# Sliding-window attention and a gated FFN on one core: VectorE's pieces given out behind the gate-value products, and the first batch's attention split between the head and the FFN

## The chip, the core and the metric

The kernel runs on one core of one Trainium2 chip. The metric is the device time of one execution in microseconds. A core has a matrix engine (TensorE, PE in the profile), VectorE (DVE), ScalarE (ACT), GpSimd (POOL) and SyncE (SP, which here only issues DMAs). Each engine runs its own instructions strictly in the order in which they were emitted, and semaphores order them across engines. Matmuls write to PSUM, which has eight banks, and VectorE and ScalarE read the results there.

## The reference

```python
# attention: batch 4, heads 8, sequence 768, head size 64; n_sink 4, window 128
scores = scale * np.matmul(q, k.transpose(0, 1, 3, 2))
keep = is_sink | ((rel >= 0) & (rel < window))      # rel = query position - key position
scores = np.where(keep, scores, -1e9)
a = softmax(scores)
attn_out = np.matmul(a, v)
# FFN: 3072 tokens, d_model 512, d_ff 1536
x = attn_out.transpose(0, 2, 1, 3).reshape(B * S, H * D)
out = (np.maximum(x @ w_gate, 0) * (x @ w_val)) @ w_out
```

A query sees at most 128 keys behind it and the first four keys. The inputs and the output are float32; the kernel multiplies in bf16.

## The kernel before

**Attention.** Two heads form a unit U[i]; a batch has four units, so there are sixteen. Four kinds of step do a unit's attention:

- `T(u)` turns the unit's keys and queries with TensorE (L228), twelve 128x128 transposes. ScalarE copies the keys to `kE` in four pieces and adds the sink keys in a fifth small copy (L233 to L238); VectorE copies the queries to `qT` (L235).
- `Sg(u, g)` computes the scores of key group g (0, 1 or 2) into a two-bank PSUM tile `PP` (L258), and ScalarE takes the exponential into `ee` (L262). The mask is either added beforehand by TensorE (L247, `bias=True`, batch 0) or multiplied in afterwards by VectorE (L264).
- `V(u, part)` multiplies the weights with the values and with ones (L276), for one half of the queries (part 0 or 1). Groups 0 and 1 serve part 0; groups 1 and 2 serve part 1.
- After V, VectorE divides: it transposes the sums (L282), takes the reciprocal (L283), transposes back (L284) and multiplies into `xT` (L286). The multiply is the last reader of V's PSUM tile.

In batches 2 and 3, DMAs turn keys and queries, so `T` is used only for batches 0 and 1.

**FFN.** `F1(b, g, m)` multiplies half g (384 tokens) of a batch with column block m of the gate weights (L302), ScalarE applies the ReLU (L305), then come the value weights (L307) and VectorE's product of gate and value into `hT` (L309). `F2(b, t)` multiplies `hT` with `wo` for 128 tokens (L318), ScalarE copies the result (L320) and a DMA stores it (L321).

**PSUM.** There are two `PP` tiles of two banks, taken in turn by `pair()`, and four single banks `G`, taken in turn by `bank()` for the FFN. In the head (`head[0]`), `two()` gives `T` and `V` two banks of `G`; afterwards it gives them a `PP` tile.

**The order of the work** is written out by hand. The head does all of batch 0's attention. Then come slots: 18 for a batch, twelve with a pair of F1 (both halves of one m; the first four slots of batch 0 pair differently) and six with an F2. The attention of batch b + 1 is put after the slots of batch b's FFN: `events(i)` makes seven steps for a pair of units, and `places` says after which slots they come. `before` holds what is emitted ahead of a slot: loads on SP, casts to bf16 on POOL (`cast_kq`, `cast_v`, `cast_w`, `cast_wo`), and for batches 2 and 3 the DMA transposes. Weights come through three staging tiles `ws`.

VectorE's masks and divisions are emitted at once, in `Sg` and in `V`:

```python
if not bias:
    nc.vector.tensor_tensor(x, x, msk..., op=Alu.mult)
```

Of the kernel before, what the change touches and what calls it, by code (L numbers as in the profile page):

```python
# [11 lines left out]
Alu = mybir.AluOpType  # L12
# [9 lines left out]
def kernel(  # L22
# [123 lines left out]
    def load_w(m0, m1):  # L146
        for w, dst in ((moe_w_gate, wg), (moe_w_val, wv)):
            st = ws[wsn[0] % NW]
            wsn[0] += 1
            n = (m1 - m0) * 128  # L150
            nc.sync.dma_start(out=st[:, 0:KO * n].rearrange("p (k n) -> p k n", n=n),
                              in_=w.rearrange("(ko ki) n -> ki ko n", ki=128)[:, :, m0 * 128:m1 * 128])
            staged[m0, dst is wv] = st

    def cast_w(m0, m1):
        n = (m1 - m0) * 128
        for m in range(m0, m1):
            for x, dst in enumerate((wg, wv)):
                st = staged[m0, x == 1]
                o = (m - m0) * 128  # L160
                nc.gpsimd.tensor_copy(dst[:, :, m * 128:(m + 1) * 128],
                                      st[:, 0:KO * n].rearrange("p (k n) -> p k n", n=n)[:, :, o:o + 128])
# [47 lines left out]
    head = [True]  # L210

    def pair():
        rot[0] += 1
        return PP[rot[0] % 2]

    def two():
        if head[0]:
            srot[0] += 2
            return G[srot[0] % 4][:], G[(srot[0] + 1) % 4][:]
        x = pair()  # L220
        return x[:, 0, :], x[:, 1, :]

    def T(u):
        t = u.i % NT
        tk, tq = two()
        for x, ps in ((kn[u.i % NC], tk), (qn[u.i % NC], tq)):
            for n in range(NR):
                nc.tensor.transpose(ps.bitcast(BF16)[:, 128 * n:128 * n + 128],  # L228
                                    x[:, n, :, :].rearrange("p h d -> p (h d)"), ident[:])
        vk, vq = (ps.bitcast(BF16)[:, 0:768].rearrange("d (n p) -> d p n", p=128) for ps in (tk, tq))  # L230
        e = kE[t]
        to = lambda ap: ap.rearrange("d (p n) -> d p n", n=NR)
        nc.scalar.copy(to(e[:, 0:126]), vk[:, 0:21])  # L233
        nc.scalar.copy(to(e[:, 130:382]), vk[:, 21:63])
        nc.vector.tensor_copy(to(qT[t][:]), vq)  # L235
        nc.scalar.copy(to(e[:, 386:638]), vk[:, 63:105])
        nc.scalar.copy(to(e[:, 642:780]), vk[:, 105:128])
        nc.scalar.copy(e[:, 126:894].rearrange("d (i c) -> d i c", c=256)[:, :, 0:4],  # L238
                       e[:, 0:4].unsqueeze(1).to_broadcast([128, 3, 4]))

    def Sg(u, g, bias=False):
        t = u.i % NT
        n, segs = SEG[g]
        ps = pair()
# [4 lines left out]
        for x0, q0, c0, c1 in segs:  # L249
            for h in range(2):  # L250
                j = X0.index(x0)
# [11 lines left out]
        if not bias:  # L263
            nc.vector.tensor_tensor(x, x, msk[:, g, 0:n].unsqueeze(1).to_broadcast([128, 2, n]), op=Alu.mult)  # L264
# [3 lines left out]
    def V(u, part):  # L268
        pv, pd = two()
        w, h0 = u.i // 2, 2 * (u.i % 2)  # L270
        segs = VSEG[part]
        for which in range(2):
            for i, (j, g, c0, c1, o0) in enumerate(segs):
                for h in range(2):
# [7 lines left out]
        nc.vector.transpose(out=t1[:], in_=pd[:, 0:CUT])  # L282
        nc.vector.reciprocal(r[:], t1[:].rearrange("p (c e) -> p c e", e=32)[:, :, 0])  # L283
        nc.vector.transpose(out=R[:].rearrange("p (c e) -> p c e", e=32),  # L284
                            in_=r[:].unsqueeze(2).to_broadcast([128, CUT // 32, 32]))
        nc.vector.tensor_tensor(xT[u.b % 2][:, u.p, CUT * part:CUT * part + CUT], pv[:, 0:CUT], R[:], op=Alu.mult)  # L286
        ready[u.b, u.p, part] = True

# [6 lines left out]
    def F1(b, g, m):  # L295
        assert all((b, p, g) in ready for p in range(NP)), (b, g)
        x = xT[b % 2]
        c = slice(CUT * g, CUT * g + CUT)
        n = CUT
        gp, vp = bank(), bank()  # L300
        for ko in range(KO):
            nc.tensor.matmul(out=gp[:, 0:n], lhsT=wg[:, ko, m * 128:(m + 1) * 128], rhs=x[:, ko, c],  # L302
                             start=ko == 0, stop=ko == KO - 1)
        gs = gspool.tile([128, S - CUT], F32, name="gs")
        nc.scalar.activation(gs[:, 0:n], gp[:, 0:n], Act.Relu, bias=0.0, scale=1.0)  # L305
        for ko in range(KO):
            nc.tensor.matmul(out=vp[:, 0:n], lhsT=wv[:, ko, m * 128:(m + 1) * 128], rhs=x[:, ko, c],  # L307
                             start=ko == 0, stop=ko == KO - 1)
        nc.vector.tensor_tensor(hT[:, m, c], gs[:, 0:n], vp[:, 0:n], op=Alu.mult)  # L309
# [13 lines left out]
    with tc.manual_schedule():  # L323
# [3 lines left out]
        for u in (1, 2):  # L327
            load_k(U[u])
            load_q(U[u])
            if u == 1:  # L330
                load_v(0, (0, 1, 2, 3))
        load_v(0, (4, 5, 6))
        cast_kq(U[0])
        T(U[0])
        Sg(U[0], 0, bias=True)
        Sg(U[0], 1, bias=True)
# [3 lines left out]
        load_v(1, range(7))  # L340
        load_w(0, 2)
        T(U[1])
        Sg(U[0], 2, bias=True)
        cast_v(0, 0, 4)
        V(U[0], 0)
        Sg(U[1], 0, bias=True)
        cast_kq(U[2])
        cast_v(0, 4, 7)
        V(U[0], 1)
        Sg(U[1], 1, bias=True)  # L350
        T(U[2])
        Sg(U[1], 2, bias=True)
        V(U[1], 0)
        Sg(U[2], 0, bias=True)
        cast_kq(U[3])
        V(U[1], 1)
        Sg(U[2], 1, bias=True)
        T(U[3])
        Sg(U[2], 2, bias=True)
        cast_v(1, 0, 4)  # L360
        V(U[2], 0)
        Sg(U[3], 0, bias=True)
        cast_v(1, 4, 7)
        cast_w(0, 2)
        load_w(2, 4)
        V(U[2], 1)
        Sg(U[3], 1, bias=True)
        V(U[3], 0)
        Sg(U[3], 2, bias=True)
        V(U[3], 1)  # L370
# [6 lines left out]
        def events(i):  # L377
# [7 lines left out]
        ffn[0][0:4] = [lambda: (F1(0, 0, 0), F1(0, 0, 1)), lambda: (F1(0, 0, 2), F1(0, 0, 3)),  # L385
                       lambda: (F1(0, 1, 0), F1(0, 1, 1)), lambda: (F1(0, 1, 2), F1(0, 1, 3))]
# [5 lines left out]
        at(0, lambda: (cast_w(2, 4), kq_in(4), load_w(4, 8)))  # L392
        at(1, lambda: (cast_kq(U[4]), kq_in(5), load_v(2, range(7))))
        at(2, lambda: cast_w(4, 8))
        at(3, lambda: load_w(8, 12))
        at(5, lambda: (cast_kq(U[5]), cast_v(2, 0, 7), kq_in(6), kq_in(7), load_v(3, range(7))))
        at(6, lambda: (cast_w(8, 12), load_wo(0), load_wo(1), load_wo(2)))
        at(9, lambda: (cast_kq(U[6])))
        at(10, lambda: (cast_v(3, 0, 7), [cast_wo(c) for c in range(3)]))
        at(12, lambda: (cast_kq(U[7]),))  # L400
# [17 lines left out]
        for b in range(1, B):  # L418
            ev = events(NP * b) + events(NP * b + 2)
            if b == 1:  # L420
                places = [3, 4, 5, 6, 7, 8, 10, 11, 12, 13, 14, 15, 16, 17]
            else:
                ev = [f for n, f in enumerate(ev) if n % 7 not in (0, 2)]
                places = [2, 3, 4, 6, 7, 9, 10, 11, 13, 14]
# [3 lines left out]
        for b in range(B):  # L428
            for f in ffn[b]:
# [3 lines left out]
                for x in after.get(s, []):  # L433
                    x()
                s += 1
# [35 lines left out]
```

## Time and profile before

| what | value |
|---|---|
| median of 3 runs | 263.98 us (263.98 to 264.33) |
| the profiled execution | 263.85 us |
| its span, first to last instruction | 261.5 us |
| mean granted TensorE clock | 0.998 |
| PE busy | 243.5 us (93%) |
| DVE busy | 149.5 us (57%) |
| ACT busy | 112.4 us (43%) |
| POOL busy | 78.3 us (30%) |
| first matmul; first F1 matmul | 6.00 us; 30.83 us |
| DMA traffic | 38.18 MB, mean 146 GB/s |

The profile is one execution; its span leaves out 2.35 us around the instructions. A row of a group names the line, the engine, the operation and its tiles, then busy time, the mean of one instruction in nanoseconds, and the idle time of the engine ahead of them with what ended most of it. In a row of waits stand the waiting line, what released it, the total in us, the number of times and the longest. In a timeline stand start, duration and instruction. Buffer numbers are left out, so both `PP` tiles are "pp" and all four banks "g".

### The profile page before, as it was taken

The page shows a single profiled execution, that of the slowest core. Times are in us where ns is not written, and L with a number is a line of the kernel's source. Part 1 is how long each engine was busy: PE and PEld are TensorE (multiplying, and loading weights), DVE is VectorE, ACT ScalarE, POOL GpSimd, SP SyncE. Part 2 cuts the span into 40 slices and gives each one's busy share as a digit, 9 for nine tenths or more (in the row PEclk, how much of TensorE's full clock was granted, in tenths as well). Part 3 has the DMA queues.
Part 4 walks back from the last instruction along what each step waited for, and adds up shares of the span by engine and source line. Part 5 has one row for each costly group of instructions (what it writes and reads, how often), then busy time and mean ns, then how long its engine had stood idle before and what let it go on. Part 6 is the DMA issues. An engine that isn't in the chain of part 4 may idle for free.

```text
span 261.5 us, 5120 instructions
## 1 busy us (share of the span) xinstructions
PE 243.5 (93%) x1988; PEld 140.2 (54%) x1988; DVE 149.5 (57%) x289; ACT 112.4 (43%) x210; POOL 78.3 (30%) x127
## 2 busy tenths in 40 slices
PE   0999699999999979998999999999999999999994
PEld 0455466665645545655554555655564556556443
DVE  4289845697835575869683525869683524444100
ACT  2667335745264426452535136453535133333211
POOL 6776558776711262135001135233000000000000
PEclk9999999999999999999999999999999999999999
DMA  6995999999289799920008989930002220000122
GB/s 231 286 285 204 363 335 309 353 292 335 39 180 243 148 231 212 165 37 3 0 3 195 224 189 231 185 70 3 1 0 83 80 80 3 0 0 3 40 107 95
DMA packets 77319, 38.18 MB, mean 146 GB/s; under 512 B 64368, under 2 KB 70768, under 8 KB 77296
## 3 DMA queue, kind: packets, MB, share of 16 engines
q1 hardware_dynamic: 76880, 37.35, 58.0%
q10 hardware_dynamic: 416, 0.52, 0.6%
q8 instruction: 15, 0.25, 0.4%
q14 instruction: 8, 0.07, 0.1%
HBM read 28.43 MB, written 6.29 MB: 133 GB/s over the span
## 4 chain that ended last, share of the span: by engine, by line
PE 74%; DVE 15%; SPq 3%; issue 2%; DMA 2%; ACT 2%; POOL 0%; DVEq 0%; ACTq 0%; POOLq 0%
PE g L318 23%; PE g L307 21%; PE g L302 20%; DVE R L284 4%; PE pp L258 4%; DVE t L282 4%; PE pp L276 4%; DVE xT L286 3%; DVE hT L309 2%; SPq L105 2%; DMA kf<-in_k_dram 2%; DVE r L283 2%; PE g L276 1%; ACT ee L262 1%; SPq L94 1%
## 5 line engine op out<-in xcount | busy, mean ns | idle before, releaser
L307 PE MATMUL g<-xT,wv 128*128 128x384 bf16 x384 | 78.1, 326 | 3.4 <-DVE hT L309 3.4
L309 DVE TENSOR_TENSOR hT<-gs,g 128x384 bf16<-128x384 f32 x96 | 51.5, 551 | 51.1 <-PE g L307 48.8
L302 PE MATMUL g<-xT,wg 128*128 128x384 bf16 x384 | 78.7, 327 | 2.0 <-DVE xT L286 1.3
L305 ACT ACTIVATE gs<-g 128x384 f32<-128x384 f32 x96 | 46.9, 493 | 71.4 <-DVE hT L309 31.5
L318 PE MATMUL g<-wo,hT 128*128 128x512 bf16 (+1 forms) x300 | 64.4, 371 | 0.0
L307 PEld LDWEIGHTS <-wv 128*128 128x128 bf16 x384 | 37.5, 98 | 30.6 <-issue 6.1
L262 ACT ACTIVATE ee<-pp 128x1010 bf16<-128x1010 f32 (+2 forms) x48 | 44.3, 964 | 12.6 <-PE pp L258 12.6
L302 PEld LDWEIGHTS <-wg 128*128 128x128 bf16 x384 | 35.8, 98 | 25.4 <-issue 2.7
L318 PEld LDWEIGHTS <-hT 128*128 128x128 bf16 x300 | 28.4, 98 | 31.0 <-issue 0.4
L264 DVE TENSOR_TENSOR ee<-ee,msk 128x1010 bf16<-128x1010 bf16 (+2 forms) x36 | 28.1, 789 | 23.0 <-ACT ee L262 22.5
L320 ACT COPY ot<-g 128x512 f32<-128x512 f32 (+1 forms) x24 | 13.8, 576 | 50.1 <-PE g L318 44.6
L117 POOL CAST kn<-kf 128x768 bf16<-128x768 f32 x16 | 13.5, 845 | 34.9 <-DMA kf<-in_k_dram 33.8
L284 DVE STREAM_TRANSPOSE R<-r 128x384 f32<-128x384 f32 x32 | 18.5, 578 | 1.1
L276 PEld LDWEIGHTS <-vn 128*64 128x64 bf16 x288 | 12.6, 110 | 8.9 <-issue 7.6
L282 DVE STREAM_TRANSPOSE t<-pp 128x384 f32<-128x384 f32 x24 | 13.8, 576 | 5.1 <-PE pp L276 4.7
L140 POOL COPY kO<-kE 128x372 bf16<-128x372 bf16 x8 | 4.4, 551 | 40.3 <-DMA kE<-kn 20.4
L258 PE MATMUL pp<-qT,kE 64*128 64x255 bf16 (+4 forms) x176 | 15.1, 255 | 1.0 <-DVE xT L286 0.8
L110 POOL CAST vn<-vf 128x1792 bf16<-128x1792 f32 (+2 forms) x10 | 13.8, 1381 | 5.6 <-DMA vf<-in_v_dram 5.6
L117 POOL CAST qn<-qf 128x768 bf16<-128x768 f32 x16 | 13.8, 862 | 5.5 <-DMA qf<-in_q_dram 4.8
L258 PEld LDWEIGHTS <-kE 64*128 64x128 bf16 x176 | 6.9, 94 | 13.4 <-issue 10.6
L286 DVE TENSOR_TENSOR xT<-pp,R 128x384 bf16<-128x384 f32 x24 | 13.4, 558 | 0.8
L276 PE MATMUL pp<-ee,vn 128*64 128x253 bf16 (+8 forms) x216 | 12.4, 236 | 0.4 <-DVE ee L264 0.4
(60 smaller groups left out, 143.8 us busy)
## 6 DMA issues: line engine op xcount, KB each, us to landing
kf<-in_k_dram SPq DMA_DIRECT2D x16, 384.0 KB, 4.8
vf<-in_v_dram SPq DMA_DIRECT2D x48, 128.0 KB, 4.3
out_dram<-ot SPq DMA_DIRECT2D x23, 256.0 KB, 2.2
qf<-in_q_dram SPq DMA_DIRECT2D x15, 384.0 KB, 5.5
ws<-in_moe_w_out_dram SPq DMA_DIRECT2D x3, 1024.0 KB
ws<-in_moe_w_gate_dram SPq DMA_DIRECT2D x2, 1024.0 KB
ws<-in_moe_w_val_dram SPq DMA_DIRECT2D x2, 1024.0 KB, 8.2
ws<-in_moe_w_gate_dram SPq DMA_DIRECT2D x2, 512.0 KB, 6.7
```

What stands on the lines that cost most here:

```text
L117: copy(dst[:], src[:].rearrange("p h (n d) -> p n h d", d=64))
L258: nc.tensor.matmul(out=ps[:, h, c0:c1], lhsT=lhs, rhs=qT[t][64 * h:64 * h + 64, q0:q0 + c1 - c0], start=not bias, stop=True, skip_group_ch ...
L262: nc.scalar.activation(x, ps[:, :, 0:n], Act.Exp, bias=0.0, scale=scale)
L264: nc.vector.tensor_tensor(x, x, msk[:, g, 0:n].unsqueeze(1).to_broadcast([128, 2, n]), op=Alu.mult)
L276: nc.tensor.matmul(out=(pv, pd)[which][64 * h:64 * h + 64, o0:o0 + c1 - c0], lhsT=lhs, rhs=ee[u.i % NE][:, g, h, c0:c1], start=i == 0, sto ...
L282: nc.vector.transpose(out=t1[:], in_=pd[:, 0:CUT])
L284: nc.vector.transpose(out=R[:].rearrange("p (c e) -> p c e", e=32), in_=r[:].unsqueeze(2).to_broadcast([128, CUT // 32, 32]))
L302: nc.tensor.matmul(out=gp[:, 0:n], lhsT=wg[:, ko, m * 128:(m + 1) * 128], rhs=x[:, ko, c], start=ko == 0, stop=ko == KO - 1)
L305: nc.scalar.activation(gs[:, 0:n], gp[:, 0:n], Act.Relu, bias=0.0, scale=1.0)
L307: nc.tensor.matmul(out=vp[:, 0:n], lhsT=wv[:, ko, m * 128:(m + 1) * 128], rhs=x[:, ko, c], start=ko == 0, stop=ko == KO - 1)
L309: nc.vector.tensor_tensor(hT[:, m, c], gs[:, 0:n], vp[:, 0:n], op=Alu.mult)
L318: nc.tensor.matmul(out=op[:, 0:c1 - c0], lhsT=hT[:, m, t * 128:(t + 1) * 128], rhs=wo[:, m, c0:c1], start=m == 0, stop=m == FM - 1)
```

## The change

- **Pieces.** VectorE's masks, the query copies of `T` and the divisions are no longer emitted at once. They go into a queue `later`; a division is two pieces, `inv` (transpose, reciprocal) and `mul` (transpose back, multiply). `some(1)` emits one piece behind every gate-value product, and `some(2)` emits two behind every slot from 12 to 17 of a batch (the F2 slots). `need(key)` emits pieces up to the one that a later step depends on: before a `PP` tile is taken again, before scores read `qT`, before V reads `ee`, before F1 reads `xT`. In the head everything is emitted at once, as before.
- **Head.** The head does `T` for all four units, one unit ahead, and only groups 0 and 1 and the first query half of each. Group 2 and the second query halves come between the F1's of the first four slots; those slots do the first half's F1 for m = 0 to 7, and the next four slots the second half's. The very first F1 works on m = 0 and 1 together, with the last of the four input blocks at the end.
- **PSUM.** `V` after the head and V(U[3], 0) use a `PP` tile; `T` after the head uses one half of each of two `PP` tiles.
- **Places.** Batch 1's fourteen steps come after slots 3 to 16 instead of 3 to 8 and 10 to 17.
- **Loads and casts.** Weights come in six pieces of 256 columns, gate and value in one staging tile, instead of pieces of 256 and 512 columns with a tile each. Several loads and casts are emitted at other slots, and the head loads U[2]'s keys and queries ahead of the first V tiles.
- **Sink keys.** The small copy within `kE` goes from ScalarE to POOL.

The diff, cut to its core:

```diff
     rot, srot = [0], [0]
     head = [True]
+    later, count, due = deque(), [0, 0], {}
+
+    def put(key, *fns):
+        for f in fns:
+            later.append(f)
+            count[0] += 1
+        for x in key:
+            due[x] = count[0]
+        if head[0]:
+            need(key)
+
+    def need(key):
+        n = max([due.get(x, 0) for x in key])
+        while count[1] < n:
+            some(1)
+
+    def some(n):
+        for _ in range(min(n, len(later))):
+            count[1] += 1
+            later.popleft()()
 
     def pair():
         rot[0] += 1
-        return PP[rot[0] % 2]
+        i = rot[0] % 2
+        need([("pp", i)])
+        return PP[i], ("pp", i)
...
     def T(u):
...
-        tk, tq = two()
+        kk = kq = None
+        if head[0]:
+            tk, tq = two()
+        else:
+            (x, kk), (y, kq) = pair(), pair()
+            tk, tq = x[:, 0, :], y[:, 0, :]
...
-        nc.vector.tensor_copy(to(qT[t][:]), vq)
+        put([("q", u.i), kq], lambda: nc.vector.tensor_copy(to(qT[t][:]), vq))
...
-        nc.scalar.copy(e[:, 126:894].rearrange("d (i c) -> d i c", c=256)[:, :, 0:4],
-                       e[:, 0:4].unsqueeze(1).to_broadcast([128, 3, 4]))
+        nc.gpsimd.tensor_copy(e[:, 126:894].rearrange("d (i c) -> d i c", c=256)[:, :, 0:4],
+                              e[:, 0:4].unsqueeze(1).to_broadcast([128, 3, 4]))
...
         if not bias:
-            nc.vector.tensor_tensor(x, x, msk[:, g, 0:n].unsqueeze(1).to_broadcast([128, 2, n]), op=Alu.mult)
+            put([("e", u.i)], lambda: nc.vector.tensor_tensor(
+                x, x, msk[:, g, 0:n].unsqueeze(1).to_broadcast([128, 2, n]), op=Alu.mult))
...
-    def V(u, part):
-        pv, pd = two()
+    def V(u, part, own=True):
+        need([("e", u.i)])
+        if own:
+            x, key = pair()
+            pv, pd = x[:, 0, :], x[:, 1, :]
+        else:
+            key = None
+            pv, pd = two()
...
+        def inv():
+            nc.vector.transpose(out=t1[:], in_=pd[:, 0:CUT])
+            nc.vector.reciprocal(r[:], t1[:].rearrange("p (c e) -> p c e", e=32)[:, :, 0])
+
+        def mul():
+            nc.vector.transpose(out=R[:].rearrange("p (c e) -> p c e", e=32),
+                                in_=r[:].unsqueeze(2).to_broadcast([128, CUT // 32, 32]))
+            nc.vector.tensor_tensor(xT[u.b % 2][:, u.p, CUT * part:CUT * part + CUT], pv[:, 0:CUT], R[:], op=Alu.mult)
+
         ready[u.b, u.p, part] = True
+        put([key, ("x", u.b, part)], inv, mul)
...
+    def F1(b, g, m, ahead=()):
...
+        need([("x", b, g)])
+        work = [(i, bank(), w) for i in (m, *ahead) for w in (wg, wv)]
...
+                    nc.vector.tensor_tensor(hT[:, i, c], gs[i][:], ps[:, 0:CUT], op=Alu.mult)
+                    some(1)
...
+        T(U[0])
+        T(U[1])
+        Sg(U[0], 0)
+        Sg(U[0], 1)
+        T(U[2])
+        Sg(U[1], 0)
+        Sg(U[1], 1)
+        V(U[0], 0, False)
+        T(U[3])
+        Sg(U[2], 0)
+        Sg(U[2], 1)
+        V(U[1], 0, False)
+        Sg(U[3], 0)
+        Sg(U[3], 1)
+        V(U[2], 0, False)
+        V(U[3], 0)
...
+        first = [lambda: (F1(0, 0, 0, (1,)), Sg(U[0], 2), Sg(U[1], 2), F1(0, 0, 2), V(U[0], 1)),
+                 lambda: (F1(0, 0, 3), Sg(U[2], 2), F1(0, 0, 4), V(U[1], 1), Sg(U[3], 2)),
+                 lambda: (F1(0, 0, 5), V(U[2], 1), F1(0, 0, 6)),
+                 lambda: (V(U[3], 1), F1(0, 0, 7))]
+        ffn[0][0:8] = first + [lambda m=m: (F1(0, 1, m), F1(0, 1, m + 1)) for m in (0, 2, 4, 6)]
...
-                places = [3, 4, 5, 6, 7, 8, 10, 11, 12, 13, 14, 15, 16, 17]
+                places = [3, 4, 5, 6, 7, 8, 9, 10, 11, 12, 13, 14, 15, 16]
...
                 for x in after.get(s, []):
                     x()
+                if s % 18 > 11:
+                    some(2)
                 s += 1
```

## The prediction

> **What bounds the kernel now.** I read the page first: engine shares, the chain that ended last, the groups.
>
> ```profile
> PE 243.5 (93%) x1988; PEld 140.2 (54%) x1988; DVE 149.5 (57%) x289; ACT 112.4 (43%) x210; POOL 78.3 (30%) x127
> PE 74%; DVE 15%; SPq 3%; issue 2%; DMA 2%; ACT 2%; POOL 0%; DVEq 0%; ACTq 0%; POOLq 0%
> L309 DVE TENSOR_TENSOR hT<-gs,g 128x384 bf16<-128x384 f32 x96 | 51.5, 551 | 51.1 <-PE g L307 48.8
> L286 DVE TENSOR_TENSOR xT<-pp,R 128x384 bf16<-128x384 f32 x24 | 13.4, 558 | 0.8
> ```
>
> TensorE carries the span; VectorE is on the chain only where TensorE waits for it. So I need TensorE's idle time and, from its timeline, where each wait falls.
>
> ```profile
> PE g L228 <- POOL kn L117: 6.0, 1, 6.0
> PE g L307 <- DVE hT L309: 3.4, 4, 1.2
> PE g L276 <- ACT ee L262: 1.4, 2, 0.8
> PE g L302 <- DVE xT L286: 1.3, 2, 0.8
> PE pp L258 <- DVE xT L286: 0.8, 2, 0.4
> ```
>
> "Idle" starts after the modelled end of a matmul, so I take lost time from starts. Four gate or value matmuls take 0.65 us from start to start; what exceeds that is lost. After 31 us: 0.46 at 59.27 (second scores wait for a division); 1.66 between 91.32 and 94.93 (batch 1's first gates wait for the last divisions); in batch 1 0.65 at 112.71 and 1.38 at 124.72 (a bank waits for a late gate-value product) and 0.43 at 119.41 (a mask); in batch 2 0.66, 0.18 and 1.37 at the same places; 0.4 at 86.89. So 7.2 us in all is what better placing of VectorE's pieces can win there. The change must keep the waits for a `PP` tile covered, and the timeline around 59 us shows how these go:
>
> ```profile
> 57.18 0.57 DVE L282 STREAM_TRANSPOSE t<-pp 128x384 f32<-128x384 f32 x1
> 57.78 0.23 DVE L283 RECIPROCAL r<-t 128x12 f32<-128x12 f32 x1
> 58.05 0.58 DVE L284 STREAM_TRANSPOSE R<-r 128x384 f32<-128x384 f32 x1
> 58.49 0.39 PE L258 MATMUL pp<-qT,kE 64*128 64x255 bf16 x4
> 58.66 0.56 DVE L286 TENSOR_TENSOR xT<-pp,R 128x384 bf16<-128x384 f32 x1
> 59.27 0.36 PE L258 MATMUL pp<-qT,kE 64*128 64x255 bf16 x6 [0.39 <-DVE xT L286]
> ```
>
> The scores at 59.27 start 0.05 after the division that read their `PP` tile ended (58.66 + 0.56). VectorE had started the two divisions as soon as V's matmuls ended, ahead of both later products.
>
> **The stall the change makes.** In the changed program's instruction order, pieces stand behind the gate-value products, and those still pending for a `PP` tile are forced out when that tile is taken again: behind the product just emitted, whose matmuls are the last on TensorE before the taker. TensorE and VectorE each run in order, so this part is serial. Steps from rows of before: the product starts 0.27 after TensorE has issued its last value matmul (40.58 + 0.65 = 41.23, product at 41.50); 0.47 until the next piece starts (the pair at 44.73 takes 1.02); `inv` (transpose, reciprocal) 0.88 (57.18 to 58.05, rounded); `mul` 0.61 until its multiply starts, which takes 0.56 and frees the tile, 0.47 until the next piece; 0.05 back to TensorE. With E the end of the value matmuls, one forced `mul` frees its tile at E + 0.27 + 0.47 + 0.61 + 0.56 = 1.91, TensorE at 1.96.
>
> - First phase (slots 0 to 3). V(U1,1) after F1(0,0,4) waits for the `mul` of V(U0,1) in the same tile: 1.96 instead of 0.08, so 1.9 lost. V(U2,1) after F1(0,0,5) waits for product, `inv`, `mul`: 2.84, so 2.75 lost. T(U4) takes both tiles after F1(0,0,7): product, `mul`, `inv`, `mul`, that is 0.27 + 0.47 + 1.08 + 0.88 + 0.61 + 0.56 + 0.05 = 3.92, where its second half would start at about 0.41: 3.5 lost. Sum 8.1.
> - Batch 0, rest. Slot 8's second scores and slot 10's T(U6) come one slot after two V's, and have the same four steps: 3.5 each. (The first product's wait is 1.3 earlier, its `inv` ends before the second product, which adds 0.05 that I leave out.) The query copies (L235, 0.96) now stand behind a slot's first product: Sg(U4,0) and Sg(U6,0) may start at (E - 1.3) + 0.27 + 0.47 + 0.96 + 0.05 = E + 0.45 instead of 0.08: 0.35 each. V(U5,1) waits for its last mask, given behind the second product (0.27 + 0.47 + 0.69 = 1.43, asked for at about 0.95): 0.45. Sum 8.2.
> - Batches 1 and 2. V to the next scores is two slots, so four products give one piece each; the last `mul` stands behind the fourth product. With F1's at 1.3: first product E - 3.63, `inv` to E - 2.28, product, `mul` to E - 0.73, product, `inv` to E + 0.62, and only then the fourth product (ready at E + 0.27), so `mul` frees the tile at E + 0.62 + 0.47 + 0.61 + 0.56 = E + 2.26. Scores there would start at E + 0.36: 1.95 lost, twice a batch. With one mask wait of 0.45: 4.35 a batch, 8.7 in both.
>
> Behind each waiting matmul stands the whole rest of TensorE's queue; exponentials and products wait with it. In the second half of batches (slots 12 to 17) no product stands between, and pieces run as now.
>
> **What it removes.** Of the 7.2 us, all but the 0.4 at 86.89 have their cause removed: products come before divisions in batches 1 and 2, V(U7) is one slot earlier so F2 covers its divisions, and 59.27's wait is the one costed anew. That is 6.8 us.
>
> **The head.** Half the scores and half the V's move behind the first products; no matmul is added or dropped. Now F1 starts at 30.83, so with its first two products TensorE would be free at 33.43. In the changed order T(U1) stands before Sg(U0,0), and POOL's small kE copy (was ACT's L238; nearest POOL row L141, 0.19) stands between the casts of two units and waits for ACT:
>
> ```profile
> 6.66 0.83 POOL L117 CAST kn<-kf 128x768 bf16<-128x768 f32 x1
> 7.54 0.31 ACT L237 COPY kE<-g 128x138 bf16<-128x138 bf16 x1
> 8.64 0.61 PE L258 MATMUL pp<-qT,kE 64*128 64x253 bf16 x4 [0.20 <-DVE qT L235]
> ```
>
> The cast at 6.66 moves to about 8.1, its partner ends at 9.7, and scores begin at about 10.4 instead of 7.39. Then ACT (exponential pair 1.84, four copies 0.85) and POOL (copy 0.2, two casts 1.6) alternate: T(U3) at about 17.4, scores of U2 and U3 to 21.6, V(U2,0) to 22.4, V(U3,0) to 23.4; divisions of U2 and U3 at 1.96 each end at 26.35, and the last input rows' matmuls of the first two products (0.65) at 27.0. The rest that stood before: four third scores at 0.73, four V's at 0.75, eight changes at 0.06: 6.4. So 33.4 against 33.43: 0. Bounds: -2.5 if POOL and ACT run tighter and TensorE's early slow time is shorter (transposes take 0.77 for six at 6.0, 0.34 from 11.28), +2.5 if the slow time lasts over the idle gap at 7.4 to 9.0, or a V tile's cast is late.
>
> **DMAs.** SP's order changes (U2's keys before V's tiles; weights as twelve 512 KB loads, gate and value of one piece in one staging tile). Bytes are the same. DMA moved 5.24 MB by 19.6 us now (three slices of 6.54 us at 231, 286 and 285 GB/s), which is what stands up to weight piece 0 in the new order; piece 1 lands at about 25, 2 at 28.6, 3 at 32, cast 2.3 later each, needed at 28.5, 32.8 and about 42. SP's load of piece 4 waits for POOL's casts of piece 1, and U4's keys behind it land at about 37, needed at 47. Cost 0, hidden by F1's and by the stalls; without the stalls piece 3 and U4 would still have several us.
>
> **Sum**, against the profiled execution's own 263.85 (span 261.5 and 2.35 around it; the median of the runs is 263.98): 263.85 + 8.1 + 8.2 + 8.7 - 6.8 + 0 = 282.05, so 282.0.
>
> **A rule beside a row.** No idle gap of TensorE after its start is longer than 1.2 us now, and after each the next four matmuls keep 0.65; the new ones reach 2.75 in one piece, and 3.5 with 0.33 of work inside. The Trainium skill, "TensorE: Matmul & The Clock Gate", section "Part 1: The HAM clock gate", says that an idle window of about 3.4 us halves the clock; the new gaps lie just under that. By the rule, if they did trip it, each would cost up to half of a window more, an estimate of 1.7 us; by the row, nothing. My sum goes by the row.
>
> **Rivals.** (1) The clock drops in the long waits: at 11.28 it came up some 5 us after the first matmul, so a drop at the five longest would cost at most 2.5 us each, more likely one or two: 284 to 288. For it: the early rows. Against: no wait here is a full stop for 3 us. (2) The head wins: 278.5 to 280, if casts and exponentials interleave better than my chain; against it, POOL's in-order wait. (3) Faster: the pieces are covered. If forced divisions were done before their taker, 25.0 falls away and 263.85 - 6.8 = 257. The point that decides: from the last value matmul to the free tile must take under 0.4 us, and the rows sum to 1.96 at the least. Only an order other than the built one would give it. (4) Waits and gains cancel: the same price per wait, a quarter of the count; I see no reason.
>
> **Chances.** Forecast (280 to 284.5) 0.70; clock or a worse head, above 284.5, 0.13; better head but still slower, 0.12; faster 0.04; no change 0.01. A difference under 0.2%, about 0.5 us, counts as none. The range 278 to 286.5 leaves out both ends of these.
>
> **What would show it.** Right: TensorE's longest waits become L285 and L253 (scores and turns, by the changed file's lines) on the division's multiply L325, about 2 and 3.5 us, three of the latter, and L311 on L325 in slots 1 and 2; products on ACT and banks on L356 vanish; F1's first matmul at 23 to 24 us, T(U4) near 49 instead of 41.2. Wrong: no waits of `pp` on L325 above 1 us, or T(U4) before 44 us.

## The result: 285.87 us, 8.3% slower

| | before | after |
|---|---|---|
| median | 264.01 us (263.98 to 264.33, 4 runs) | 285.87 us (284.47 to 288.03, 4 runs) |
| profiled execution | 263.85 us | 284.85 us |
| its span | 261.5 us | 283.1 us |
| its mean granted clock | 0.998 | 0.986 |

The ratio after to before is 1.083 (95% interval 1.075 to 1.091). The four runs of the changed kernel lie much further apart than those before, and in the order of their clocks: 284.47 us at 0.987, 284.85 at 0.986, 286.88 at 0.979, 288.03 at 0.976.

**Busy time and clock.** The page of the changed kernel: engine shares, the granted clock in 40 slices of 7.1 us, and the chain that ended last.

```profile
PE 248.5 (88%) x1988; PEld 141.7 (50%) x1988; DVE 144.8 (51%) x289; ACT 112.0 (40%) x202; POOL 79.5 (28%) x135
PEclk9999999799998999999999999999999999999999
PE 71%; DVE 19%; DMA 4%; issue 3%; POOL 1%; ACT 0%; SPq 0%; DVEq 0%; POOLq 0%; ACTq 0%
```

VectorE has the same 289 instructions and is busy for less time than before, but its share of the chain goes from 15% to 19%. The clock row shows a 7 and an 8; in the kernel before it is this:

```profile
PEclk9999999999999999999999999999999999999999
```

**TensorE's waits** (line, releaser, total us, times, longest):

```profile
PE pp L285 <- DVE xT L325: 10.0, 7, 1.8
PE g L253 <- POOL kn L117: 7.2, 2, 6.0
PE pp L253 <- DVE xT L325: 6.5, 4, 1.8
PE pp L311 <- DVE xT L325: 4.5, 2, 2.7
PE pp L311 <- DVE ee L291: 1.0, 3, 0.4
PE g L348 <- DVE xT L325: 1.0, 2, 0.8
PE pp L285 <- DVE qT L260: 0.3, 1, 0.3
```

L285, L253 and L311 are scores, turns and V; L325 is the division's multiply. All three wait for it, 21.0 us together in 13 waits; before, scores and V had three short waits for a division, 1.0 us together. The old waits for a gate-value product (3.4 us on L307) have no row left; the product is now L356.

**One turn.** VectorE's timeline ahead of the second half of T(U4), which is TensorE's row at 49.63:

```profile
45.98 0.56 DVE L356 TENSOR_TENSOR hT<-gs,g 128x384 bf16<-128x384 f32 x1 [0.92 <-PE g L348]
46.46 0.57 DVE L323 STREAM_TRANSPOSE R<-r 128x384 f32<-128x384 f32 x1
47.06 0.56 DVE L325 TENSOR_TENSOR xT<-pp,R 128x384 bf16<-128x384 f32 x1
47.54 0.57 DVE L319 STREAM_TRANSPOSE t<-pp 128x384 f32<-128x384 f32 x1
48.14 0.23 DVE L320 RECIPROCAL r<-t 128x12 f32<-128x12 f32 x1
48.41 0.58 DVE L323 STREAM_TRANSPOSE R<-r 128x384 f32<-128x384 f32 x1
49.02 0.56 DVE L325 TENSOR_TENSOR xT<-pp,R 128x384 bf16<-128x384 f32 x1
```

And TensorE's timeline around it:

```profile
45.06 0.81 PE L348 MATMUL g<-xT,wv 128*128 128x384 bf16 x4
47.67 0.49 PE L253 MATMUL pp<-ident,kn 128*128 128x128 bf16 x6 [1.80 <-DVE xT L325]
49.63 0.57 PE L253 MATMUL pp<-ident,qn 128*128 128x128 bf16 x6 [1.46 <-DVE xT L325]
49.99 1.48 PE L348 MATMUL g<-xT,wg 128*128 128x384 bf16 x4
51.27 1.48 PE L348 MATMUL g<-xT,wv 128*128 128x384 bf16 x4
```

Product, `mul`, `inv`, `mul` run one behind another and TensorE starts 0.05 us after each multiply. What follows was not in the forecast's sum: the next four gate matmuls take 1.28 us from start to start (49.99 to 51.27) where four take 0.65 elsewhere. The windows view of the changed kernel gives the clock for that (window, its length, busy time and instructions of PE, PEld, DVE, ACT, POOL, then the granted clock, DMA share, GB/s):

```profile
47.00:49.60 2.60, 0.49 (x6) 0.38 (x6) 2.44 (x6) 0.99 (x4) 0.48 (x2) 1.00 1.00 344
49.60:53.00 3.40, 3.37 (x16) 1.81 (x16) 0.14 (x1) 0.49 (x1) 3.34 (x5) 0.55 1.12 344
84.60:88.00 3.40, 3.40 (x16) 1.66 (x14) 0.51 (x2) 0.49 (x1) 0.65 (x1) 0.58 0.00 0
```

In the stretch of T(U4)'s waits full clock is granted (1.00), behind them about half (0.55). The same happens behind T(U6). In slices of 0.1 us the same view shows half clock from 49.92 to 53.33 and from 84.05 to 87.47 us, 3.41 us each (the hundredths come from the mean clock of the slice in which it changes). The six query transposes and the twelve gate and value matmuls behind each turn take 3.96 us (49.63 to 53.59) and 3.94 (84.03 to 87.97) by their starts, where 0.33 for the six and 0.1625 for each of the twelve, 2.28 together, is the full pace. So they lose 1.68 + 1.66 = 3.34 us.

**By stretch**, from the starts of the first F1 or F2 of each batch in both timelines:

| stretch | before | after | difference | the forecast's terms |
|---|---|---|---|---|
| start to first F1 of batch 1 | 91.32 | 110.70 | +19.38 | 8.1 + 8.2 - 0.46 = +15.84 |
| F1 of batch 1 | 43.36 | 43.12 | -0.24 | 4.35 - 1.66 - 2.46 = +0.23 |
| F1 of batch 2 | 41.21 | 43.04 | +1.83 | 4.35 - 2.21 = +2.14 |
| all F2 of batches 1 and 2, F1 of batch 3 | 66.62 | 66.62 | 0.0 | 0 |

The differences sum to 20.97, the forecast's terms to 18.21. Without the 3.34 us at half pace, all of it in the first stretch, 17.63 are left. The F2 of batch 3, to the end of the span, takes 0.63 us longer (18.99 to 19.62), and what lies outside the span is 0.60 shorter (2.35 to 1.75), so the two executions differ by 21.00.

### The profile page after: what moved, and what is told of

Same layout as the page of the kernel before. It is cut to its first block, busy times and chain, and to the rows that moved or that the text cites. A ratio compares the mean times of both kernels' runs of the same rounds, so it can differ in the third digit from the quotient of the medians.

```text
span 283.1 us, 5137 instructions
## 1 busy us (share of the span) xinstructions
PE 248.5 (88%) x1988; PEld 141.7 (50%) x1988; DVE 144.8 (51%) x289; ACT 112.0 (40%) x202; POOL 79.5 (28%) x135
## 4 chain that ended last, share of the span: by engine, by line
PE 71%; DVE 19%; DMA 4%; issue 3%; POOL 1%; ACT 0%; SPq 0%; DVEq 0%; POOLq 0%; ACTq 0%
PE g L348 37%; PE g L366 21%; PE pp L311 6%; DVE hT L356 6%; PE pp L285 4%; DVE R L323 4%; DVE t L319 3%; DVE xT L325 3%; DMA vf<-in_v_dram 2%; DMA qf<-in_q_dram 2%; DVE ee L291 2%; PE pp L274 1%; DVE r L320 1%; PE pp L253 1%; PE g L311 1%
## 5 line engine op out<-in xcount | busy, mean ns | idle before, releaser
L356 DVE TENSOR_TENSOR hT<-gs,g 128x384 bf16<-128x384 f32 x96 | 52.7, 550 | 89.5 <-PE g L348 72.1
L348 PE MATMUL g<-xT,wg 128*128 128x384 bf16 x384 | 80.7, 332 | 1.0 <-DVE xT L325 1.0
L348 PE MATMUL g<-xT,wv 128*128 128x384 bf16 x384 | 79.8, 330 | 0.0
L291 DVE TENSOR_TENSOR ee<-ee,msk 128x1010 bf16<-128x1010 bf16 (+2 forms) x36 | 25.9, 720 | 11.7 <-ACT ee L289 11.6
L285 PE MATMUL pp<-qT,kE 64*128 64x255 bf16 (+4 forms) x176 | 15.3, 252 | 10.3 <-DVE xT L325 10.0
L117 POOL CAST kn<-kf 128x768 bf16<-128x768 f32 x16 | 13.5, 845 | 32.7 <-DMA kf<-in_k_dram 32.7
L311 PE MATMUL pp<-ee,vn 128*64 128x138 bf16 (+8 forms) x264 | 15.5, 236 | 5.7 <-DVE xT L325 4.5
L285 PEld LDWEIGHTS <-kE 64*128 64x128 bf16 x176 | 7.5, 94 | 23.4 <-issue 21.8
L311 PEld LDWEIGHTS <-vn 128*64 128x64 bf16 x288 | 12.8, 110 | 12.7 <-issue 12.6
L319 DVE STREAM_TRANSPOSE t<-pp 128x384 f32<-128x384 f32 x29 | 16.7, 576 | 4.0 <-PE pp L311 4.0
L325 DVE TENSOR_TENSOR xT<-pp,R 128x384 bf16<-128x384 f32 x29 | 16.2, 557 | 1.0
L117 POOL CAST qn<-qf 128x768 bf16<-128x768 f32 x16 | 13.6, 851 | 5.7 <-DMA qf<-in_q_dram 5.5
L311 PE MATMUL pp<-ee,ones 128*64 128x138 bf16 (+8 forms) x264 | 14.3, 233 | 0.0
```

Source lines behind the costliest of these rows:

```text
L117: copy(dst[:], src[:].rearrange("p h (n d) -> p n h d", d=64))
L285: nc.tensor.matmul(out=ps[:, h, c0:c1], lhsT=lhs, rhs=qT[t][64 * h:64 * h + 64, q0:q0 + c1 - c0], start=not bias, stop=True, skip_group_ch ...
L291: put([("e", u.i)], lambda: nc.vector.tensor_tensor(x, x, msk[:, g, 0:n].unsqueeze(1).to_broadcast([128, 2, n]), op=Alu.mult))
L311: nc.tensor.matmul(out=(pv, pd)[which][64 * h:64 * h + 64, o0:o0 + c1 - c0], lhsT=lhs, rhs=ee[u.i % NE][:, g, h, c0:c1], start=i == 0, sto ...
L348: nc.tensor.matmul(out=ps[:, 0:CUT], lhsT=w[:, ko, i * 128:(i + 1) * 128], rhs=x[:, ko, c], start=ko == 0, stop=ko == KO - 1)
L356: nc.vector.tensor_tensor(hT[:, i, c], gs[i][:], ps[:, 0:CUT], op=Alu.mult)
```

## Experiments

The theory: pieces emitted behind the last product are forced out while TensorE waits for them, and those waits are the loss; behind some of the longest the clock falls, and that is the rest. Rivals: the new head and order cost the time; or the pieces cost it by their number and not by their place; and for the clock, that something else than the waits brings it down.

### Pieces emitted at once, all else as changed

```diff
             due[x] = count[0]
-        if head[0]:
-            need(key)
+        need(key)
```

> The changed kernel, but every mask, query copy and division is emitted at once, as before; the new head, places, loads and PSUM use stay. Theory A (the time is lost because pieces stand behind the last gate-value product ahead of the taker of their tile): the waits of TensorE on the division's multiply fall from 21 us to about 2, the clock drops go with them, and what is left is the new head and places: 263.85, less 1.66 at the turn to batch 1, less 0.4 in the head, plus 0.46 and 0.25 for turns that now come one slot behind V: 262.5 (261.5 to 264). Rival B (the loss is in the split head, its loads and POOL's copy in the cast queue): 280 or more.

Measured: 264.33 us (263.76 to 266.37, 10 runs) beside 264.22; ratio 1.001 (0.999 to 1.003), clock 1.0. TensorE's waits of this kernel, whose lines stand one lower than in the changed kernel (L347 value matmuls, L252 turns, L284 scores):

```profile
PE g L347 <- DVE hT L355: 3.4, 4, 1.2
PE pp L252 <- DVE xT L324: 1.2, 2, 0.6
PE pp L284 <- DVE xT L324: 0.7, 2, 0.4
```

The waits of 1.8 us and the half pace are gone, and before's waits for a product are back. So the whole loss is in the giving out, and the new head, order and loads together are worth nothing that can be told from 0. The time lies 1.8 us over the centre that was expected, and 0.3 over its range: F1 of batch 1 is 1.72 shorter, as the wait at its start is gone, but it begins at 93.39 us, 2.07 later than before. T(U4) starts 0.61 later (41.84 for 41.23), and the second halves of T(U4) and T(U6) wait 0.59 and 0.57 us for a division, where before neither waited.

### Giving out alone, in the old order

The queue, `need` and `some` as in the changed kernel, put into the kernel before; its head, slots, places and loads stay.

```diff
         nc.vector.tensor_tensor(hT[:, m, c], gs[:, 0:n], vp[:, 0:n], op=Alu.mult)
+        some(1)
```

> The kernel before, with only the giving out of pieces; head, places, loads, casts and the small copy are as before. Theory A: waits of 3.5 us at the scores and at the turn that stand one slot behind a V in batch 0, 1.15 for query copies and one mask, 4.35 in each of batches 1 and 2 in place of 2.46 and 2.21: 263.85 + 3.05 + 3.5 + 1.15 + 8.7 - 4.67 = 275.6, and one clock drop at the turn of up to 1.7: 275.5 to 278. Rival B: within 2 us of 264.

Measured: 277.2 us (276.21 to 279.32, 4 runs); ratio 1.050 (1.044 to 1.056), clocks 0.982 to 0.992. Waits of this kernel (L281 scores, L333 gate matmuls, L250 turns), and one of its gate matmuls:

```profile
PE pp L281 <- DVE xT L314: 10.0, 7, 1.8
PE g L333 <- DVE xT L314: 3.0, 2, 2.2
PE pp L250 <- DVE xT L314: 1.8, 1, 1.8
105.19 0.32 PE L333 MATMUL g<-xT,wg 128*128 128x384 bf16 x1 [2.19 <-DVE xT L314]
```

The theory held in its total: the same 10.0 us in seven waits of scores are here, without the changed kernel's first phase. Its terms are not all right. T(U6) waits once, 1.79 us, where 3.5 was expected; batch 1's first gates, expected as before, wait 0.83 and 2.19. Some 2.6 and 1.7 us at half pace come on top in the profiled execution, from 62.0 and 106.4 us, behind slot 8's scores and behind the wait of 2.19, not behind the turn as expected.

### One piece ahead of the product instead of behind it

```diff
                 else:
-                    nc.vector.tensor_tensor(hT[:, i, c], gs[i][:], ps[:, 0:CUT], op=Alu.mult)
                     some(1)
+                    nc.vector.tensor_tensor(hT[:, i, c], gs[i][:], ps[:, 0:CUT], op=Alu.mult)
```

> The changed kernel with one edit: one piece is given out ahead of each gate-value product instead of behind it. Theory A, by the same steps: in batches 1 and 2 every division is done before the fourth product, so these waits go. Where a taker comes one slot behind V, two pieces are still forced behind the last product: 0.27 + 0.47 + 0.88 + 0.61 + 0.56 + 0.05 = 2.84 instead of 0.41 at T(U4), at slot 8 and at T(U6), 2.4 lost each, and 1.9 at V(U2,1), nothing at V(U1,1): 9.1. The version with two ahead had about 3.1 at these places and measured 261.8, so 267.8, and up to 2 more if the clock falls: 267 to 270. Rival (the side of the product does not matter, only the number of pieces): 280 or more.

Measured: 270.34 us (268.84 to 271.69, 4 runs); ratio 1.024 (1.019 to 1.028); the lowest at clock 0.999, the others at 0.985 to 0.991. Waits of this kernel:

```profile
PE pp L285 <- DVE xT L325: 4.0, 7, 2.0
PE pp L253 <- DVE xT L325: 2.8, 2, 2.3
PE pp L311 <- DVE xT L325: 1.8, 1, 1.8
```

The same pieces, as many per product, moved across one instruction, give back 15.5 us: it is the place, not the number. The median lies 0.3 us over the range that was expected. A fourth wait, 1.93 us at T(U6)'s query half, stands in the view under a cast on POOL; the division's multiply ends 0.05 us ahead of it (75.75 + 0.56, start at 76.36), as ahead of the others.

### Two pieces ahead of the product

```diff
                 else:
+                    some(2)
                     nc.vector.tensor_tensor(hT[:, i, c], gs[i][:], ps[:, 0:CUT], op=Alu.mult)
-                    some(1)
```

> The changed kernel with one edit: two pieces are given out ahead of each gate-value product instead of one behind it. Theory A: a whole division then runs while the value matmuls of the next F1 run, so forced pieces are rare; what is left is about 0.75 at each of the two places of batch 0 that come one slot behind V and 0.25 at the first turn, and the 6.8 us of waits of the kernel before are gone: 263.85 - 6.8 - 0.4 + 1.75 = 258.4 (257.5 to 260.5). Rival B: 280 or more. Rival D (a piece ahead of a product makes the product late, and banks wait for it): 262 to 266, with waits of the gate or value matmuls on the product of 4 us or more.

Measured: 261.82 us (261.66 to 263.9, 9 runs); ratio 0.992 (0.989 to 0.995). Faster than before, but 3.4 us over the centre that was expected and 1.3 over its range. Waits of this kernel:

```profile
PE pp L253 <- DVE xT L325: 1.6, 2, 1.0
PE pp L285 <- DVE xT L325: 1.4, 2, 1.1
PE g L348 <- DVE hT L357: 0.7, 2, 0.4
```

F1 of batch 1 takes 40.20 us and of batch 2 39.78, that is 3.16 and 1.43 less than before; but batch 1 begins at 93.80, 2.48 later than before. What is left is in the head and batch 0: with one slot or less between V and the step that takes its tile, two pieces ahead of a product aren't early enough. The second halves of T(U4) and T(U6) and slot 8's second scores wait 0.59, 1.04 and 1.05 us; with pieces at once it is 0.59, 0.57 and 0.35. Beside that kernel, which has the same head and places, giving out two ahead gains 2.5 us (264.33 to 261.82).

### Two ahead for the later batches only

The kernel before with its own head and batch 0, pieces at once there; only the attention of batches 2 and 3, which lies in the FFN of batches 1 and 2, is given out. Batch 1's places are 3 to 16, with U[7]'s casts one slot earlier.

```diff
-        if head[0]:
+        if not defer[0]:
             need(key)
...
+        some(2)
         nc.vector.tensor_tensor(hT[:, m, c], gs[:, 0:n], vp[:, 0:n], op=Alu.mult)
...
         for b in range(B):
+            defer[0] = b > 0
```

> The kernel before with the head, loads and batch 0 as they were, divisions and masks of batch 1's attention emitted at once, and only those of batches 2 and 3 given out, two pieces ahead of a product; the fourteen places of the attention after batch 0's slots as in the changed kernel. Theory A: the waits of batches 1 and 2 fall from 4.67 to about 1.2, the 1.66 at the turn to batch 1 goes, and the turn one slot behind V costs 0.5: 264.1 - 3.5 - 1.66 + 0.5 = 259.5 (258.5 to 261). Rival B (the new head is what gains): 262 or more.

Measured: 260.19 us (259.91 to 261.56, 4 runs); ratio 0.986 (0.983 to 0.989), clock 1.0. It held, and this is the fastest version here. Waits of this kernel (L282 scores, L339 value matmuls):

```profile
PE pp L282 <- DVE xT L315: 1.2, 2, 0.8
PE g L339 <- DVE hT L342: 1.0, 3, 0.4
PE pp L302 <- DVE ee L288: 0.4, 1, 0.4
```

F1 of batches 1 and 2 take 40.63 and 39.77 us, 2.73 and 1.44 less than before, and the waits for a product go from 3.4 to 1.0 us. Not all of it comes from the pieces: the new places alone, in the run with pieces at once, made F1 of batch 1 1.72 us shorter. About 1.0 us in batch 1 and 1.4 in batch 2 are left for giving out two ahead, an estimate across two kernels, and batch 1 begins 0.87 later than before.

### The clock: unused matmuls in the turns' gap

Eight matmuls of 384 columns into a spare bank, between the key and the query half of T(U4) and T(U6), in the changed kernel.

```diff
         for x, ps in ((kn[u.i % NC], tk), (qn[u.i % NC], tq)):
+            if ps is tq and u.i in (NP, NP + 2):
+                spare = G[(gn[0] + 1) % 4]
+                for _ in range(8):
+                    nc.tensor.matmul(out=spare[:, 0:CUT], lhsT=ident[:], rhs=msk[:, 1, 0:CUT], start=True, stop=True,
+                                     skip_group_check=True)
```

> The changed kernel with eight matmuls of 384 columns added between the two halves of the turns T(U4) and T(U6), into a bank that the next F1 overwrites; their results are not used. They take 1.3 us and lie within a wait of 1.46. Theory C (a turn with waits on both sides lets the clock fall, since it is little or no matmul work): the half-speed matmuls behind these turns, 1.65 and 1.4 us of loss in the profiled run, vanish, and the time falls by about 3 to 282 (281 to 283), with a mean clock of 0.997 instead of 0.986. Rival: the slow matmuls have another cause (weights, contention): no gain, 285 to 287.

Measured: 286.81 us (283.25 to 287.16, 4 runs); 0.980, 0.994, 0.980 and 0.981 in clock. The expected 281 to 283 was missed; only one run came near it, at 0.994. Behind both filled turns full pace is kept (four gate matmuls take 0.65 us from 52.06 and from 87.81), but the time did not come down, so the fall does not belong to the turns as such. TensorE's timeline shows that it moved:

```profile
41.98 0.86 PE L317 MATMUL pp<-ee,vn 128*64 128x121 bf16 x10 [2.68 <-DVE xT L331]
42.64 0.88 PE L317 MATMUL pp<-ee,ones 128*64 128x121 bf16 x10
43.45 1.46 PE L352 MATMUL g<-xT,wg 128*128 128x384 bf16 x4
73.31 0.53 PE L291 MATMUL pp<-qT,kE 64*128 64x255 bf16 x6 [1.56 <-DVE xT L331]
73.77 1.46 PE L352 MATMUL g<-xT,wg 128*128 128x384 bf16 x4
```

Here V(U2,1) at 41.98 and slot 8's scores are followed by half pace. The changed kernel has the same two waits, and behind them the full one:

```profile
41.34 0.52 PE L311 MATMUL pp<-ee,vn 128*64 128x121 bf16 x9 [2.68 <-DVE xT L325]
42.17 0.82 PE L348 MATMUL g<-xT,wg 128*128 128x384 bf16 x4
72.55 0.36 PE L285 MATMUL pp<-qT,kE 64*128 64x255 bf16 x6 [1.56 <-DVE xT L325]
72.84 0.82 PE L348 MATMUL g<-xT,wg 128*128 128x384 bf16 x4
```

So a wait of 2.7 us, or 1.8 and 1.6 with a short burst between, can bring the clock down and need not. The next four runs leave the changed kernel out and ask for the length alone.

### The clock: a wait of one length, in the kernel before

N unneeded VectorE transposes ahead of a gate-value product, at four places of batch 3 (this is N = 4).

```diff
+        if b == B - 1 and g == 0 and m in (2, 5, 8, 11):
+            for _ in range(4):
+                t = npool.tile([128, CUT], F32, name="R")
+                nc.vector.transpose(out=t[:], in_=gs[:, 0:n])
         nc.vector.tensor_tensor(hT[:, m, c], gs[:, 0:n], vp[:, 0:n], op=Alu.mult)
```

> The kernel before with four transposes of 128x384 added on VectorE ahead of one product at four places of the last batch's F1 (m = 2, 5, 8, 11; nothing else runs there); their results are not used. TensorE should wait about 1.2 us at each for its bank: 264.2 + 4.8 = 269. Theory C2 (the clock falls only when a wait is near 3 us): no slow matmuls in that stretch, mean clock as before (0.998 to 1.000). Rival C3 (any repeated wait does it): slow stretches of 1 us or more, 271 or more.

> As the kernel with short delays, but seven transposes at each of the four places: waits of about 3 us each, 264.2 + 12.2 = 276.4 without the clock. Theory C2: behind some of the four, matmuls run at half speed for up to 3.4 us, so single runs scatter from 276.5 to 281 and the mean clock lies between 0.975 and 0.995, lower where the time is longer. Rival (the slow stretches of the changed kernel belonged to turns, scores or weights): 276 to 277, clock 0.998 or more.

> The kernel before with nine unneeded transposes of the gate tile on VectorE ahead of the gate-value product at four places of batch 3 (slots of m = 2, 5, 8, 11, first half). Seven of them gave waits of 1.79 us at three places and no lower clock; each more adds 0.48 us, so about 2.7 us of wait at three places, and 264.1 + 3 x 2.9 = 272.8 us if only the waits cost time. Theory (the clock comes down behind a wait of somewhat under 3 us, by where the wait lies, as behind the 2.7 us wait of the second query half's V in the changed kernel): clock under 0.997 in some of the runs and their times 1 to 3 us above 272.8; others at 272.8. Rival (length alone does nothing here; it takes two waits with a short burst between them): clock 0.998 to 1.000 in every run, all within 0.6 us of each other.

> The same with eleven transposes: about 3.7 us of wait at three places, and 264.1 + 3 x 3.9 = 275.7 us if only the waits cost time. Theory: clock 0.975 to 0.995 in all or nearly all runs, stretches of matmuls at half pace behind at least one of the waits, and 1 to 5 us on top. Rival: clock 0.998 to 1.000 in every run and times within 0.6 us of each other near 275.7.

| N | wait, at three places | time (4 runs each) | clock of the runs |
|---|---|---|---|
| 4 | 0.41 us | 265.88 us (265.47 to 266.29) | 1.000 in all |
| 7 | 1.79 us | 270.28 us (270.1 to 270.77) | 1.000 in all |
| 9 | 2.71 us | 275.51 us (274.67 to 277.69) | 1.000, 0.992, 0.992, 0.986 |
| 11 | 3.63 us | 281.73 us (280.91 to 282.61) | 0.988, 0.988, 0.982, 0.982 |

With four and seven the waits, and so the times, came out below what was expected (269 and 276.4 us), since transposes overlap each other; that made them a test of 1.8 us, not of 3. With nine, the profiled execution took 274.67 us at clock 1.000 against 272.8 for the bare sum; 0.99 of that is a wait within the first F2 of batch 3 that the sum lacked, and 0.6 a later first cast (6.6 for 6.0). The wait of 2.7 us that the expectation names had half pace behind it in the run with added matmuls, not in the changed kernel's trace. With eleven, TensorE's timeline at the first two places, and the windows ahead of the first place, ahead of the third and behind the third:

```profile
224.44 1.44 PE L307 MATMUL g<-xT,wv 128*128 128x384 bf16 x4 [3.63 <-DVE hT L313]
225.67 1.48 PE L302 MATMUL g<-xT,wg 128*128 128x384 bf16 x4
238.77 0.81 PE L307 MATMUL g<-xT,wv 128*128 128x384 bf16 x4 [3.63 <-DVE hT L313]
```

```profile
220.60:224.40 3.80, 0.21 (x2) 0.00 (x0) 3.80 (x10) 0.49 (x1) 0.00 (x0) 0.84 0.00 0
246.60:250.30 3.70, 0.13 (x1) 0.00 (x0) 3.70 (x10) 0.49 (x1) 0.00 (x0) 1.00 0.00 0
250.30:254.00 3.70, 3.64 (x13) 1.70 (x13) 1.02 (x3) 0.49 (x1) 0.00 (x0) 0.54 0.02 4
```

Three equal waits of 3.63 us: matmuls are at half pace behind the first and the third, not behind the second, and at the first the clock falls before the wait has ended (0.84). The theory held: length is enough, from somewhere between 1.8 and 3.6 us, and where the fall comes is not set by the wait alone. All four times lie above the range that was expected, 276.7 to 280.7, since the sum of 275.7 lacked a wait of 1.91 us within the first F2 of batch 3. At 2.71 us it is less sure: 0.992 also shows in 2 of the 32 runs of the kernel before whose clock is on record beside these, but 0.986 in none.

**Where the fall comes.** The traces of these runs show what picks one wait and not another. In slices of 0.1 us, the clock of a profiled execution falls at times that lie 34.14 us apart (changed kernel), 27.31 (eleven transposes), 30.72 (added matmuls) and 44.37 (giving out alone): 10, 8, 9 and 13 times 3.413. Half clock lasts 3.41 us or twice that. So the clock changes on a grid of 3.413 us, which does not follow the waits. Counted on that grid, TensorE's idle time (window less busy time) is:

| execution | grid window, us | idle in it, us | clock behind it |
|---|---|---|---|
| changed kernel | 36.27 to 39.68, 39.68 to 43.09 (the 2.68 wait) | 1.01, 1.66 | full |
| changed kernel | 46.51 to 49.92 (T(U4)) | 2.63 | half to 53.33 |
| changed kernel | 66.98 to 70.40, 70.40 to 73.81 (slot 8) | 1.60, 1.75 | full |
| changed kernel | 80.64 to 84.05 (T(U6)) | 2.89 | half to 87.47 |
| added matmuls | 38.31 to 41.72 (the 2.68 wait) | 2.42 | half to 45.14 |
| added matmuls | 69.03 to 72.44 (slot 8) | 2.49 | half to 79.27 |
| eleven transposes | 219.81 to 223.22 (first wait) | 2.41 | half to 230.05 |
| eleven transposes | 233.46 to 236.88, 236.88 to 240.29 (second wait) | 1.73, 1.89 | full |
| eleven transposes | 247.12 to 250.53 (third wait) | 3.24 | half to 253.94 |
| giving out alone | 58.61 to 62.02 (slot 8) | 1.89 | half to 68.85 |
| giving out alone | 102.98 to 106.39 (the 2.19 wait) | 2.19 | half to 109.81 |

Every fall stands behind a window with at least 1.89 us of idle time, and no window without a fall has more than 1.90, past the first 12 us of these four executions. (At the start matmuls are slow though the view shows full clock.) The run with one piece ahead, whose last fall at 266.75 gives its grid, has waits of up to 2.34 us, no window over 1.67 between 12 us and its last matmul, and no fall there. So about 1.9 us of idle time within one grid window is the limit here, and the same wait passes or fails by where it lies on the grid. This is read from traces; no run moved a wait along the grid. By an estimate from it, a wait of 2.71 us should bring the clock down at two places of three, and the clocks of the four runs with nine speak for fewer; that is open.

## Why the prediction was right, and what it put at the wrong size

The forecast was 282.05 us, and the median of 285.87 is 3.8 above it. It lies inside the range of 278 to 286.5 by 0.6 us, but outside the 280 to 284.5 that was given a chance of 0.70, and two of the four runs (286.88 and 288.03) lie above the range. The waits were forecast well; that the number still fell inside owes something to which falls of the clock the four runs happened to have.

- **What bounds the kernel, and the serial steps:** right. The forced `mul` starts and ends in the rows at 46.46 to 47.06 and 48.41 to 49.02 as the forecast built it from rows of before, and TensorE's waits of 1.80, 2.68 and 1.80 + 1.46 us are its 1.9, 2.75 and 3.5 less the end of a matmul.
- **First phase and batch 0:** 15.84 forecast, 16.04 measured without the half pace. T(U4) was put near 49, and its two halves started at 47.67 and 49.63; slot 8 and T(U6) show two waits each with 0.3 us of work between, as said. The mask wait is 0.32 us; of the two waits for a query copy one is left, 0.27 us.
- **Head:** put at 0 with 2.5 either way. Its marks came 0.3 to 1.4 us early: scores at 10.13 for 10.4, T(U3) at 15.95 for 17.4, and the first two products' matmuls issued at 26.6 for 27.0. With pieces at once and with two ahead, T(U4) starts at 41.84 and 41.06 us for 41.23 before. The rival that the head wins fell.
- **Batches 1 and 2:** right within 0.5 us each; scores wait 1.58 and 1.57 us in batch 1, in the places named.
- **What it removes:** right. The turn into batch 1 at 110.70 has no wait, and no product or bank wait is left. What the forecast did not look for is the order that keeps this: two ahead of the product in batches 1 and 2, with the new places, makes a kernel that is 1.4% faster. Its condition for a faster kernel, that forced pieces be done before their taker, was the right one, but the best time is 260.19 us, not the 257 of its third rival.
- **DMAs at 0:** nothing speaks against it; no row of TensorE's waits names a transfer, and casts (L117) hold it up only in the head.
- **The clock, at 0:** this is the term that was mis-sized. It measured 3.34 us in the profiled execution; a line through the fastest and the slowest of the four runs, (288.03 - 284.47) / (0.987 - 0.976) or 3.2 us for 0.01 of clock, reaches 281 us at before's 0.998, so by this estimate it is 3 to 7 us by run. The step that failed is "by the row, nothing": the row was a wait of 1.2 us, and it was carried over to waits of 2.7 and 3.5. The runs with added transposes show that single waits of 1.8 us do nothing either, and 3.6 us does. The Trainium skill's rule ("TensorE: Matmul & The Clock Gate", "Part 1: The HAM clock gate") warned in the right direction, and the forecast's estimate from it, up to 1.7 us per fall, is near the 1.68 and 1.66 measured at two; where half clock lasted two windows, as from 62.02 to 68.85 us with giving out alone, it was too low (some 2.6). Taken as a threshold the rule would still have misled: an idle time of 1.9 us within a window of 3.41 is enough here, also in two waits with 0.3 us of matmuls between. The section also says that the window runs free; the grid of 3.413 us in the traces, on which equal waits of 3.63 us have different outcomes, agrees.
- **Rival 1**, the clock drops at one or two of the long waits, 284 to 288 us: this is what happened, on top of the forecast's sum. That no wait is a full stop of 3 us is true (2.68 is the longest), but it does not keep the clock up.

Not settled: why 2.71 us brought the clock down so seldom, and the falls in two runs of the kernel before, of which there is no trace.

## What to carry to other kernels

On an engine that works in order, side work must be emitted ahead of the instruction that waits for the critical engine, not behind it: the same pieces cost 21.5 us one behind the product (285.87 against 264.33 at once), 6.0 us one ahead of it (270.34), and gain 2.5 us two ahead of it (261.82). When waits are added, find out how long the bound engine will stand still within a stretch of 3.4 us, short bursts of work taken out, and don't carry a row of a short wait over to a longer one. Give work out only where there is slack for it; where the taker comes one step later, emit it at once.

## What the runs showed of the hardware

- TensorE's granted clock changed on a grid of 3.413 us in four traces: falls 10, 8, 9 and 13 such steps apart, half clock for one step or two (3.41 or 6.83 us).
- It fell behind grid windows with at least 1.89 us of idle time and kept up behind windows with at most 1.90. It can fall within a wait: at 223.22 us, 1.22 before the first wait of 3.63 us ended.
- By the mean clock, three waits of 3.63 us brought it down in all four runs (0.982 to 0.988), of 2.71 us in one (0.986) and perhaps three of four, and of 1.79 us in none (1.000).
- A burst of 0.3 us of matmuls between two waits of 1.8 and 1.5 us did not prevent it; with eight matmuls of 384 columns in the gap of a turn no fall came at either turn of one trace.
- One grid step at half clock cost 1.66 to 1.68 us. The changed kernel's four runs lie 3.6 us apart, in the order of their clocks.
- VectorE's 128x384 float32 transposes overlap: ten take 4.67 us in one row of the run with eleven, where a single one takes 0.57 to 0.58.
